# Windowed attention with sink keys, then routed experts: scores and V products in four 64x64 tiles over the halves of keys that each half of queries sees

## The chip, the cores and the metric

One core of a Trainium2 chip runs the whole program. The time is that of the device for one execution, in microseconds; the kernel before has 536.01 us as the median of 3 runs. In the profile PE is TensorE's matrix product, PEld its weight loads, DVE is VectorE, ACT is ScalarE, POOL is GpSimd and SP is SyncE, which issues most DMAs.

## What is computed

There are 4 batches, 8 heads, 768 positions and 64 elements in a head. A query sees the first 4 keys (the sinks) and the 128 keys up to itself. The attention's output is regrouped to 3072 tokens of 512 elements, and each token goes through the one expert of 8 that its largest gate logit names.

```python
scores = scale * np.matmul(q, k.transpose(0, 1, 3, 2))
is_sink = pos[None, :] < int(n_sink)
rel = pos[:, None] - pos[None, :]
in_window = (rel >= 0) & (rel < int(window))
scores = np.where(is_sink | in_window, scores, -1000000000.0)
...
out = np.matmul(a, v)                  # a: softmax of the scores
...
logits = x @ w_gate
e_idx = np.argmax(logits, axis=1)
...
h = np.maximum(x[mask] @ w1[e], 0.0)
out[mask] = gate_w[mask, None] * eom[mask, e, None] * (h @ w2[e])
```

## The kernel before

Two heads of a batch make a pair (index `a` in the code); there are 16 pairs, and `pair(p)` records one. Its 128 partitions hold head 0 in the lower half and head 1 in the upper. The 768 positions are six tiles of 128 queries.

For each tile `t`, `score(t)` (line 1227) has TensorE compute the scores of 128 queries against 260 key columns: 128 of the tile before, 4 sinks, 128 of its own tile. Tile 0 needs 132 columns. Each head is one matmul in a 64-row tile of the array, all 128 queries wide, plain fp32 (which the engine runs as two instructions). `fold` on VectorE (lines 1234 to 1239) puts the scores of the tile before into the places of the own tile's future keys and takes the row maximum; `exps` on ScalarE (line 1243) takes the exponentials, 132 columns a head. `trans(j)` transposes two tiles of them on TensorE (line 1267), ScalarE copies them out of PSUM (line 1270) into `f`, and GpSimd splits them by two selects into `f` (keys of the own tile) and `g` (keys of the tile before).

`av(kt)` (line 1318) is the V product of one tile of keys: its `f` part goes to the queries of tile `kt`, its `g` part to those of tile `kt + 1`, with all 128 keys as rows and a 64-column tile of the array for each head. The outputs of query tiles 0 to 3 lie in the PSUM bank `oA`, those of 4 and 5 in `oB`. The sinks go a way of their own: GpSimd packs their exponentials (line 1287), TensorE transposes them (1293), ScalarE rounds them to the fast fp32 form (1302) and VectorE takes what rounding left (1296); three DMAs put high, high and low parts on 24 rows of `psk` (1306), which `av_sink` (1330) multiplies by a likewise split copy of the sink values, `vst` (1199, 1200, once a batch). ScalarE then copies `oA` and `oB` to `ot` (1334, 1335); the gate product (1340) writes into the rest of `oB` and is copied to `lgT` (1344); `ot` is transposed back and divided by the row sums (1380, 1383).

After each batch VectorE routes its tokens. Four early expert slots take full slots of the batches that are done, the first in plain fp32 (line 1057), the others with weights split in high and low parts (1076, 1114). Thirteen more follow when all batches are routed. Weights come in chunks of 512 KB.

No loop runs on the chip in this part: a planner (`Plan.order`) decides the order of every engine's instructions before. Each step has an engine, a guessed length, its dependences and a due number, which is the pair's base plus the table `AT`, or the entry of the table `PIN` for that step alone. On each engine the step that can start first goes, and among those near it the one with the smallest due number. `SWITCH` is the planner's guess for TensorE's change of tile shape, `SOFT` how far a plain expert step may be put off. What the planner puts out is fixed; on the chip each engine goes through its own list and waits on semaphores. The score buffers are two (`s0`, `s1`), so the scores of tile `t + 2` wait for the exponentials of tile `t`.

Of the kernel before, what the change touches and what calls it, by code (L numbers as in the profile page):

```python
# [8 lines left out]
F32 = mybir.dt.float32  # L9
# [41 lines left out]
SOFT = 11611  # L51
# [5 lines left out]
    "load": -121675, "v": -30283, "vs": 194803, "sinkv": -43076, "scale0": 12478, "scale1": -125988, "scale2": 94931,  # L57
    "s0": 3034, "s1": 8110, "s2": 8849, "s3": 12417, "s4": 3772, "s5": 8559, "fold": -17871, "exp": 28702,
    "tr0": 32076, "tr1": 44886, "tr2": 55920, "trc": 52551, "mask": 31852, "pack": -44418, "guard": -99464,
# [72 lines left out]
}  # L132


# [1526 lines left out]
```

## Time and profile before

| what | value |
|---|---|
| median of 3 runs | 536.01 us (535.85 to 536.72) |
| profiled execution | 534.44 us, its span 532.6 us |
| TensorE granted clock, mean | 0.990 |
| busy: PE, PEld, DVE, ACT, POOL | 500.5, 389.9, 346.3, 283.0, 196.6 us |
| moved | 113.01 MB, mean 212 GB/s |

A record of the profile lasts from an instruction's start until its result has landed, so a matmul's record holds the drain of the array, and records of one block lie over each other. Attention lasts until about 200 us: the last score matmul starts at 185.1 us. A timeline row merges neighbouring records of one line (x4 is four of them); one plain fp32 matmul makes two records. A row's bracket says how long the engine was idle before it and what ended that.

### The profile page before, as it was taken

What the parts mean: (1) busy time and instruction counts of PE and PEld (TensorE: products, weight loads), DVE (VectorE), ACT (ScalarE), POOL (GpSimd) and SP (SyncE); (2) the same over time, 40 slices, a digit from 0 to 9 for tenths busy, and PEclk for the clock granted to TensorE, in tenths of its full rate; (3) what the DMA queues carried; (4) which work ended last, traced back from release to release, by engine and by line L of the source; (5) the groups of instructions that cost most, each with busy time, mean ns of one, the idle gap of its engine ahead of it and who ended that gap; (6) DMA issues with size and microseconds to landing.
All of it is one profiled execution on the core that took longest, in us unless ns stands there. A gap on an engine that the chain in (4) does not pass through costs nothing.

```text
span 532.6 us, 10377 instructions
## 1 busy us (share of the span) xinstructions
PE 500.5 (94%) x3501; PEld 389.9 (73%) x3501; DVE 346.3 (65%) x800; ACT 283.0 (53%) x741; POOL 196.6 (37%) x298
## 2 busy tenths in 40 slices
PE   8799999998899989997999899999998999999992
PEld 3556676666566766687898898979886986988861
DVE  6567788788876495979999752163546578274530
ACT  4477777676756544763545432261626567365420
POOL 8675867767683253024053203040205012001101
PEclk9899999999999999999999899999999999999998
DMA  8454456536991219594385834865499979984860
GB/s 268 113 166 149 157 161 185 159 109 226 387 333 49 61 46 298 186 313 176 120 303 187 286 113 153 311 238 179 156 352 343 293 271 293 380 279 147 287 231 21
DMA packets 62687, 113.01 MB, mean 212 GB/s; under 512 B 8188, under 2 KB 28928, under 8 KB 62626
## 3 DMA queue, kind: packets, MB, share of 16 engines
q1 hardware_dynamic: 58162, 98.13, 54.5%
q0 software_dynamic: 4464, 14.14, 7.7%
q8 instruction: 30, 0.49, 0.4%
q14 instruction: 31, 0.25, 0.1%
HBM read 98.48 MB, written 13.44 MB: 210 GB/s over the span
## 4 chain that ended last, share of the span: by engine, by line
PE 43%; issue 25%; DVE 10%; DMA 8%; POOL 6%; ACT 4%; SPq 1%; POOLq 0%; another core or an unknown queue 0%; ACTq 0%; DVEq 0%
PE s L1076 13%; PE oA L1114 7%; PE oB L1114 5%; PE s L1227 5%; DMA q<-in_qT_dram 3%; PE oA L1318 3%; PE tp L1267 2%; ACT e L1243 2%; POOL out_dram L970 2%; DMA v<-in_vx_dram 2%; DMA raw<-in_w_dram 2%; PE s L1057 2%; POOL xg L892 2%; PE tp L1380 1%; DMA xg<-xd,idx_e 1%
## 5 line engine op out<-in xcount | busy, mean ns | idle before, releaser
L1243 ACT ACTIVATE e<-s,nmx 128x132 f32<-128x132 f32 x192 | 69.7, 371 | 37.8 <-DVE nmx L1239 28.4
L970 POOL DMA_INDIRECT out_dram<-y,idx x20 | 20.9, 1043 | 137.1 <-ACT y L967 133.7
L1227 PE MATMUL s<-k,q 64*128 64x260 f32 (+1 forms) x384 | 65.4, 412 | 4.9 <-ACT e L1243 4.4
L988 ACT ACTIVATE hh<-s 128x512 fp32r<-128x512 f32 (+1 forms) x36 | 23.2, 644 | 74.8 <-PE s L1076 65.8
L991 DVE SCALAR_TENSOR_TENSOR hl<-s,hh 128x512 fp32r<-128x512 f32 (+1 forms) x36 | 26.9, 747 | 50.7 <-ACT hh L988 50.7
L892 POOL DMA_INDIRECT xg<-xd,idx x21 | 27.5, 1309 | 85.0 <-PE tp L952 45.3
L1227 PEld LDWEIGHTS s<-k,q 64*128 64x128 f32 x384 | 33.4, 189 | 22.5 <-ACT e L1243 15.0
L1236 DVE COPY_PREDICATED s<-maskf,s 128x256 f32<-128x256 int32 x80 | 33.8, 423 | 17.9 <-PE s L1227 13.0
L1239 DVE TENSOR_REDUCE nmx<-s 128x2 f32<-128x264 f32 x96 | 41.5, 432 | 3.3
L1208 POOL TENSOR_SCALAR q<-q 128x256 f32<-128x256 f32 x45 | 38.0, 861 | 7.7 <-DMA q<-in_qT_dram 2.7
L383 POOL TENSOR_SCALAR_AFFINE_SELECT g<-f 128x512 f32<-128x512 f32 (+1 forms) x48 | 26.9, 560 | 33.1 <-ACT f L1270 33.0
L1243 ACT ACTIVATION_READ_ACCUMULATOR e<-s,nmx 128x1 f32 x192 | 38.8, 202 | 0.0
L1270 ACT COPY f<-tp 128x512 f32<-128x512 f32 x48 | 28.0, 588 | 11.0 <-PE tp L1267 10.9
L1267 PE MATMUL tp<-ident,e 128*128 128x128 f32 x192 | 30.1, 284 | 0.9 <-DVE x L1383 0.7
L1318 PE MATMUL oA<-f,v 128*64 128x128 f32 x256 | 26.8, 288 | 2.7 <-DMA v<-in_vx_dram 2.7
L383 POOL TENSOR_SCALAR_AFFINE_SELECT f<-f 128x512 f32<-128x512 f32 (+1 forms) x48 | 27.7, 576 | 3.3
L1267 PEld LDWEIGHTS tp<-ident,e 128*128 128x128 f32 x192 | 21.5, 143 | 9.5 <-issue 2.7
L1318 PEld LDWEIGHTS oA<-f,v 128*64 128x64 f32 x256 | 14.5, 137 | 11.9 <-issue 8.3
L967 ACT ACTIVATE y<-oA,sc 128x512 f32<-128x512 f32 (+1 forms) x18 | 11.7, 650 | 20.3 <-PE oA L1114 14.8
L970 POOL DMA_INDIRECT out_dram<-y,idx_e x8 | 9.9, 1242 | 32.1 <-ACT y L967 30.5
L1318 PE MATMUL oA<-g,v 128*64 128x128 f32 x192 | 18.9, 276 | 0.0
L931 DVE TENSOR_TENSOR wa1l<-raw,wa1h 128x1024 fp32r<-128x1024 f32 x11 | 13.4, 1223 | 7.5 <-ACT wa1h L927 7.4
(550 smaller groups left out, 1530.9 us busy)
## 6 DMA issues: line engine op xcount, KB each, us to landing
raw<-in_w_dram SPq DMA_DIRECT2D x96, 512.0 KB
v<-in_vx_dram SPq DMA_DIRECT2D x8, 768.0 KB
xd<-x SPq DMA_DIRECT2D x16, 384.0 KB
k<-in_kx_dram SPq DMA_DIRECT2D x15, 396.0 KB
q<-in_qT_dram SPq DMA_DIRECT2D x15, 384.0 KB
wa0h<-in_w_dram SPq DMA_DIRECT2D x3, 512.0 KB
wa0l<-in_w_dram SPq DMA_DIRECT2D x3, 512.0 KB
wa3h<-in_w_dram SPq DMA_DIRECT2D x3, 512.0 KB
```

Source lines behind the costliest of these rows:

```text
L383: nc.gpsimd.affine_select(out=ap, in_=ap if src is None else src, pattern=pattern, compare_op=op, fill=fill, base=base, channel_multiplier=cm)
L892: nc.gpsimd.indirect_dma_start(out=p.get(key), out_offset=None, in_=xd[0:n + 1, :], in_offset=bass.IndirectOffsetOnAxis(ap=ids(), axis=0))
L970: nc.gpsimd.indirect_dma_start(out=where, out_offset=bass.IndirectOffsetOnAxis(ap=ids(), axis=0), in_=p.get(yk)[:, 0:m], in_offset=None, b ...
L1076: nc.tensor.matmul(out=p.get(ps)[:, j, 0:cols], lhsT=a, rhs=p.get(x)[:, d, 0:cols], start=d == 0 and i == 0, stop=d == ND - 1 and i == 2)
L1114: nc.tensor.matmul(out=p.get(ys[s]), lhsT=h[a][:, s * P:(s + 1) * P], rhs=w[b_], start=f == 0 and i == 0, stop=f == NF - 1 and i == len(th ...
L1208: (nc.gpsimd if p else nc.vector).tensor_scalar(out=c, in0=c, scalar1=SCALE, scalar2=None, op0=ALU.mult)
L1227: nc.tensor.matmul(out=get(s)[:, a, o0:P + CW], lhsT=get(q)[r, t * P:(t + 1) * P], rhs=get(k)[r, k0:k0 + P + CW - o0], start=True, stop=True)
L1236: nc.vector.copy_predicated(out=both[:, :, 4:CW], mask=bc(maski[:, 1, 4:CW], 1, 2), data=z[:, :, 0:P])
L1239: nc.vector.tensor_reduce(out=get(nmx)[:, t, :], in_=both, axis=AX.X, op=ALU.max, negate=True)
L1243: nc.scalar.activation(out=get(e)[:, t, a, :], in_=get(s)[:, a, P:P + CW], func=AF.Exp, bias=get(nmx)[:, t, a:a + 1], scale=1.0, accum_out ...
L1267: nc.tensor.transpose(out=get(tp)[:, i, :], in_=get(e)[:, 2 * j + i // 2, i % 2, 4:CW], identity=ident)
L1318: nc.tensor.matmul(out=o, lhsT=v_[:, kt, p % 2 * P + a * D:p % 2 * P + (a + 1) * D], rhs=src[:, kt, a, :], start=t == kt == 0 or t == kt + ...
```

## The change

`score` computes each tile with t > 0 in four 64x64 tiles of the array, two heads by two halves of 64 queries, and over 196 columns each: the lower half of queries leaves out the upper 64 keys of its own tile, and the upper half the lower 64 of the tile before. The score buffers become two lasting PSUM tiles, written once at the start.

The V product has rows of 64 keys. Each tile of keys gives `f` and `g` products for each half of keys; two of these four cover all 128 queries and two only the 64 that see the half. A query tile with an even number now lies in `oA`, one with an odd number in `oB`, three of each. The products go in six parts: three "even" ones, in which the lower half of rows writes `oA` and the upper `oB`, then three "odd" ones the other way round. Between them ScalarE copies one column of `oB` to `tick`, after the even parts; the odd parts wait for it.

The sinks stay plain fp32: two packings, two transpositions, one copy of 256 columns, two DMAs, and four products of 384 columns in 64x64 tiles. The low part and its VectorE steps go, and the sink values are loaded straight into `vst`. The gate product writes both banks, three matmuls of 128 columns in each. All of `AT` and `PIN` are new, and `SWITCH` and `SOFT` with them.

```diff
-SOFT = 11611
+SOFT = 12779
...
-    "load": -121675, "v": -30283, "vs": 194803, "sinkv": -43076, "scale0": 12478, "scale1": -125988, "scale2": 94931,
+    "load": -118603, "v": -35855, "vs": 192361, "scale0": 15699, "scale1": -134944, "scale2": 109581, "s0": 1473,
...
-    SWITCH = {"row": 200}
+    SWITCH = {"four": 170}
...
+        class Held:
+            def __init__(self):
+                self.tiles = {}
+            def tile(self, shape, dt, name):
+                if name not in self.tiles:
+                    self.tiles[name] = ps.tile([P, 2, 512], F32, name=name)
+                t = self.tiles[name]
+                return t if len(shape) == 3 else t[:, 0, :]
...
-                nc.vector.tensor_copy(out=vst[0:24], in_=get(vsr))
-                tt(out=vst[0:8], in0=get(vsr)[0:8], in1=vst[0:8].bitcast(F32), op=ALU.subtract)
+                    def sink_values(r=slice(i * D, i * D + 2 * SINK)):
+                        nc.sync.dma_start(out=vsts[b % 2][r], in_=vs[b, 0:2 * SINK])
...
-                    for a in range(2):
-                        r = slice(a * D, (a + 1) * D)
-                        nc.tensor.matmul(out=get(s)[:, a, o0:P + CW], lhsT=get(q)[r, t * P:(t + 1) * P],
-                                         rhs=get(k)[r, k0:k0 + P + CW - o0], start=True, stop=True)
+                    for h in range(2):
+                        c0, c1 = (o0, P + CW) if t == 0 else (0, P + CW - D) if h == 0 else (D, P + CW)
+                        for a in range(2):
+                            r = slice(a * D, (a + 1) * D)
+                            nc.tensor.matmul(out=get(s)[h * D:(h + 1) * D, a, c0:c1], lhsT=get(q)[r, t * P + h * D:t * P + (h + 1) * D],
+                                             rhs=get(k)[r, k0 + c0 - o0:k0 + c1 - o0], start=True, stop=True)
...
-            pl.op("DVE", fn=sink_lo, r=[st_, (hl, 0)], w=[(hl, 1)], at=(at, "lo"), **dve(128))
-            for j, w in enumerate((0, 0, 1)):
+            for j in range(2):
...
+            parts = [("even", 0, 1), ("even", 2, 3), ("even", 4, 5), ("odd", 4, 5), ("odd", 0, 1), ("odd", 2, 3)]
+            def av(i):
+                side, *kts = parts[i]
+                todo, ks = [], set()
+                for kt in kts:
+                    whole = (kt % 2 == 0) == (side == "even")
+                    for h, src, t in ((0, "f", kt), (1, "g", kt + 1)) if whole else ((0, "g", kt + 1), (1, "f", kt)):
+                        if t < T:
+                            todo.append((h, src, kt, t, (0, P) if whole else ((0, D), (D, P))[h]))
...
+                    for h, src, kt, t, (c0, c1) in todo:
+                        rows_ = slice(h * D, (h + 1) * D)
+                        for a in range(2):
+                            o = get((oA, oB)[t % 2])[a * D:(a + 1) * D, t // 2, c0:c1]
...
+                    pl.op("ACT", fn=lambda: nc.scalar.copy(out=get(tick), in_=get(oB)[:, 2, 0:1]), r=[oA, oB, ("av", p, 1), ("av", p, 2)],
+                          w=[tick], at=(at, "tick"), **act(1))
...
-                for o, t0, t1 in ((get(oA)[:, 1:4, :], 0, 3), (get(oB)[:, 0:2, :], 3, 5)):
-                    nc.tensor.matmul(out=o, lhsT=vsts[b % 2][:, hp, :], rhs=psks[p % 2][:, t0:t1, :],
+                for r, o in ((slice(0, D), oB), (slice(D, P), oA)):
+                    for a in range(2):
+                        c = slice(a * D, (a + 1) * D)
+                        nc.tensor.matmul(out=get(o)[c, 0:3, :], lhsT=vsts[b % 2][r, hp, c], rhs=psks[p % 2][r],
```

The order, too, is another. TensorE's list of the kernel before, from the last two of the nine groups of one pair's V product (1318) and its sinks (1330) on; line 1227 is the scores, 1293 the sinks' transposition, 1380 that of `ot`, 1340 the gate product:

```order
L1318 MATMUL oB<-g_587,v_238 64x128 x2
L1318 MATMUL oB<-f_582,v_238 64x128 x2
L1330 MATMUL oA<-psk_189,vst_190 128x384
L1330 MATMUL oB<-psk_189,vst_190 128x256
L1227 MATMUL s_768<-k_490,q_481 128x132 x2
L1227 MATMUL s_774<-k_490,q_481 128x260 x2
L1293 MATMUL tp_783<-ident,pk_772 40x128
L1380 MATMUL tp_785<-ident,ot_777 128x128 x4
L1318 MATMUL oA<-f_726,v_238 64x128 x2
```

The same list of the kernel after, around the step from even to odd parts of one pair; its line 1335 is the V product, 1232 the scores, 1272 the transposition of exponentials:

```order
L1335 MATMUL oA<-f_450,v_240 64x128 x2
L1335 MATMUL oB<-g_468,v_240 64x128 x2
L1335 MATMUL oB<-f_450,v_240 64x64 x2
L1232 MATMUL s_212<-k_234,q_229 64x196 x4
L1272 MATMUL tp_655<-ident,e_530 128x128 x4
L1232 MATMUL s_209<-k_345,q_342 64x132 x4
L1335 MATMUL oB<-g_468,v_240 64x64 x2
L1335 MATMUL oA<-f_450,v_240 64x64 x2
L1335 MATMUL oB<-f_450,v_240 64x128 x2
```

The V product that ran through without a break is cut in two, and two score blocks and a transposition stand in the cut.

ScalarE's list of the kernel after at the same place; line 1248 is the exponentials, 1275 the copy of transposed ones, 1348 the tick:

```order
L1248 ACTIVATE e_530,rs_531<-s_209,nmx_512 128x132 x2
L1348 COPY tick_664<-oB 128x1
L1275 COPY f_636<-tp_655 128x512
L1248 ACTIVATE e_530,rs_531<-s_212,nmx_512 128x132 x2
L1248 ACTIVATE e_708,rs_709<-s_209,nmx_682 128x132 x2
```

The tick, which the list before does not have, stands behind one pair of exponentials and ahead of the copy and the exponentials that answer to the work in the cut.

SyncE's list of the kernel before, up to the first weight load of the first early slot; `q`, `k`, `v` are queries, keys and values, line 1306 sends the packed sinks, `order_i` names the expert:

```order
L1185 DMA q_1824<-in_qT_dram 128x768
L1185 DMA k_1831<-in_kx_dram 128x792
L1306 DMA psk_189<-hlk_1887 8x5x128 x3
L1190 DMA v_1932<-in_vx_dram 128x6x256
L897 TENSOR_LOAD order_i
L897 ISA x2
L915 ISA
L915 DMA wa0h<-in_w_dram 128x1024
```

And of the kernel after, up to the same load; line 1313 sends the packed sinks, 1421 stores an output:

```order
L1313 DMA psk_189<-hlk_2284 8x3x128 x2
L895 TENSOR_LOAD order_i
L895 ISA x2
L1421 DMA xd<-x_2320 128x6x128
L1191 DMA q_2377<-in_qT_dram 128x768
L1191 DMA k_2379<-in_kx_dram 128x792
L913 ISA
L913 DMA wa0h<-in_w_dram 128x1024
```

The loads of one more pair's queries and keys now stand ahead of those weights. Before, the loads of two pairs stood behind all eight of them, now those of one.

## Rows read from the trace of the kernel before

**Rows 1.** Windows, whole core: length, PE, PEld, DVE, ACT, POOL busy, clock, DMA.

```profile
20.00:120.00 100.00, 95.87 (x925) 64.43 (x924) 77.32 (x221) 72.20 (x301) 68.35 (x121) 1.00 0.47 146
120.00:160.00 40.00, 35.81 (x348) 24.47 (x349) 32.27 (x97) 26.09 (x110) 30.46 (x50) 1.00 0.91 315
...
300.00:500.00 200.00, 198.42 (x1151) 170.71 (x1149) 105.70 (x128) 96.52 (x138) 32.06 (x27) 1.00 0.72 254
```

**Rows 2.** Timeline (start, length, engine): TensorE around one V product.

```profile
107.12 0.66 PE L1267 MATMUL tp<-ident,e 128*128 128x128 f32 x4
...
107.70 0.71 PE L1227 MATMUL s<-k,q 64*128 64x260 f32 x4
...
108.34 0.20 PEld L1318 LDWEIGHTS oA<-f,v 128*64 128x64 f32 x4 [0.34 <-issue]
108.34 0.44 PE L1318 MATMUL oA<-f,v 128*64 128x128 f32 x4
...
108.61 0.39 PE L1318 MATMUL oA<-g,v 128*64 128x128 f32 x4
108.72 0.25 PEld L1318 LDWEIGHTS oA<-f,v 128*64 128x64 f32 x4
...
108.83 0.39 PE L1318 MATMUL oA<-f,v 128*64 128x128 f32 x4
...
109.05 0.39 PE L1318 MATMUL oA<-g,v 128*64 128x128 f32 x4
...
109.38 0.30 PEld L1227 LDWEIGHTS s<-k,q 64*128 64x128 f32 x4 [0.18 <-ACT e L1243]
```

**Rows 3.** Waits of weight loads, 20 to 200: total, times, longest.

```profile
PEld s L1227 <- ACT e L1243: 13.6, 35, 1.2
...
PEld tp L1293 <- POOL pk L1287: 3.4, 6, 1.1
```

**Rows 4.** Timeline: the two sink products of one pair.

```profile
101.01 0.44 PE L1330 MATMUL oA<-psk,vst 64*128 64x384 f32 x1
...
101.29 0.28 PE L1330 MATMUL oB<-psk,vst 64*128 64x256 f32 x1
```

**Rows 5.** Timeline, 101 to 105: the steps that change on other engines.

```profile
101.27 0.24 POOL L1287 COPY pk<-e 128x40 f32<-128x40 f32 x1
...
101.61 0.41 DVE L1199 CAST vst<-vsr 24x512 fp32r<-24x512 f32 x1
...
102.05 0.68 DVE L1200 TENSOR_TENSOR vst<-vsr,vst 8x512 fp32r<-8x512 f32 x1
...
102.49 0.26 ACT L1302 CAST hlk<-tp 40x128 fp32r<-40x128 f32 x1
...
102.77 2.33 SPq L1306 DMA_DIRECT2D psk<-hlk  x3
...
103.50 0.37 ACT L1344 COPY lgT<-oB 96x256 f32<-96x256 f32 x1 [0.76 <-PE oB L1340]
...
104.12 0.27 DVE L1296 TENSOR_TENSOR hlk<-tp,hlk 40x128 fp32r<-40x128 f32 x1
```

**Rows 6.** Timeline: one pair of exponentials on ScalarE.

```profile
108.48 0.40 ACT L1243 ACTIVATE e<-s,nmx 128x132 f32<-128x132 f32 x1
...
108.83 0.40 ACT L1243 ACTIVATE e<-s,nmx 128x132 f32<-128x132 f32 x1
...
109.09 0.24 ACT L1243 ACTIVATION_READ_ACCUMULATOR e<-s,nmx 128x1 f32 x1
```

**Rows 7.** Windows of line 1227 alone: length, PE busy (records), PEld.

```profile
20.00:120.00 100.00, 39.89 (x236) 20.26 (x236) 1.00 0.47 146
```

**Rows 8.** Chain of waits, 126 to 160: start, length; then TensorE's timeline before 18.

```profile
134.14 9.93 DMA q<-in_qT_dram
...
16.67 0.69 PE L1318 MATMUL oA<-f,v 128*64 128x128 f32 x4 [2.71 <-DMA v<-in_vx_dram]
```

More of the change, by code (lines that the diff above doesn't have):

```diff
@@ L1172, in idle, with begin @@
                 nc.tensor.matmul(out=pl.get(spare), lhsT=ones, rhs=bc(ones, 1, 4), start=True, stop=True)
-        pl.op("PE", 2400, lambda: idle(7), w=[spare], at=-1000000, mode="full", busy=2400)
+        whole = [new(pl, "s", [P, 2, 512], key=("warm", i)) for i in range(2)]
+        def begin():
+            for t in whole:
+                for i in range(2):
+                    nc.tensor.matmul(out=pl.get(t)[:, i, :], lhsT=ones, rhs=bc(ones, 1, 4), start=True, stop=True)
+            idle(3)
+        pl.op("PE", 2400, begin, w=[spare, *whole], at=-1000000, mode="full", busy=2400)
         def pair(p):
@@ L1282, in pair, with pack, fn @@
                 trans(j)
-            pk, hl = new(pl, "pk", [P, 2, SINK, T - 1], key=("pk", p)), new(pl, "hlk", [8 * (T - 1), 2, P], F32R, key=("hlk", p))
-            st_, n = new(pl, "tp", [P, P], key=("sk", p)), 8 * (T - 1)
-            def pack():
-                nc.gpsimd.tensor_copy(out=get(pk), in_=get(e)[:, 1:T, :, 0:4].rearrange("p t a s -> p a s t"))
+            n = SINK * T
+            pk = new(pl, "pk", [P, 2, n], key=("pk", p))
+            hl, st_ = new(pl, "hlk", [n, 2, P], key=("hlk", p)), new(pl, "tp", [P, 2, P], key=("sk", p))
+            def pack(j):
+                def fn():
+                    nc.gpsimd.tensor_copy(out=get(pk)[:, j, :].rearrange("p (a s t) -> p a s t", a=2, s=SINK),
+                                          in_=get(e)[:, 1 - j:T:2, :, 0:SINK].rearrange("p t a s -> p a s t"))
+                pl.op("POOL", fn=fn, r=[(e, t) for t in every], w=[(pk, j)], at=(at, "pack"), took=250, busy=420)
             def guard():
@@ L1292, in turn_sink @@
             def turn_sink():
-                nc.tensor.transpose(out=get(st_)[0:n, :], in_=get(pk).rearrange("p a s t -> p (a s t)"), identity=ident)
-            def sink_lo():
-                tt(out=get(hl)[:, 1, :], in0=get(st_)[0:n, :], in1=get(hl)[:, 0, :].bitcast(F32), op=ALU.subtract)
+                for j in range(2):
+                    nc.tensor.transpose(out=get(st_)[0:n, j, :], in_=get(pk)[:, j, :], identity=ident)
             every = range(T)
-            pl.op("POOL", fn=pack, r=[(e, t) for t in every], w=[pk], at=(at, "pack"), took=250, busy=420)
+            for j in range(2):
+                pack(j)
@@ L1308, in pair, with send @@
+            pl.op("ACT", fn=lambda: nc.scalar.copy(out=get(hl), in_=get(st_)[0:n]), r=[st_], w=[hl], at=(at, "hl"), **act(256))
+            for j in range(2):
+                def send(j=j):
+                    nc.sync.dma_start(out=psks[p % 2][j * D:j * D + 2 * SINK], in_=get(hl)[:, j, :])
+                pl.op("SP", 2000, send, r=[hl], w=[(("psk", p % 2), j)], at=(at, "send"), size=20000, busy=790)
             pl.op("DVE", fn=lambda: nc.vector.reciprocal(out=get(rs), in_=get(rs)), r=[(rs, "g")], w=[(rs, "r")], at=(at, "recip"), **dve(12))
@@ L1324, in pair @@
-            for kt in range(T):
-                av(kt)
+            parts = [("even", 0, 1), ("even", 2, 3), ("even", 4, 5), ("odd", 4, 5), ("odd", 0, 1), ("odd", 2, 3)]
[7 more added lines that the diff above has]
+                            todo.append((h, src, kt, t, (0, P) if whole else ((0, D), (D, P))[h]))
+                            ks.add(((f, g)[src == "g"], t // 2))
+                def fn():
+                    for h, src, kt, t, (c0, c1) in todo:
+                        rows_ = slice(h * D, (h + 1) * D)
+                        for a in range(2):
+                            o = get((oA, oB)[t % 2])[a * D:(a + 1) * D, t // 2, c0:c1]
+                            nc.tensor.matmul(out=o, lhsT=get(v)[rows_, kt, p % 2 * P + a * D:p % 2 * P + (a + 1) * D],
+                                             rhs=get((f, g)[src == "g"])[rows_, kt, a, c0:c1], start=i == 0 and kt == 0,
+                                             stop=False, skip_group_check=True)
+                ks = sorted(ks, key=str)
+                cost = pe(325, "four")
+                if i == 0:
+                    return pl.op("PE", fn=fn, r=ks + [v], w=[oA, oB], at=(at, "av0"), **cost)
+                return pl.op("PE", fn=fn, r=ks + [v] + [("tick", p)] * (i > 2), w=[("av", p, i)], hold=[oA, oB], behind=begun, at=(at, "av%d" % i), **cost)
@@ L1326, in pair @@
+            begun = [av(0)]
+            for i in range(1, 6):
+                if i == 3:
+                    tick = new(pl, "tick", [P, 1], key=("tick", p))
+                    pl.op("ACT", fn=lambda: nc.scalar.copy(out=get(tick), in_=get(oB)[:, 2, 0:1]), r=[oA, oB, ("av", p, 1), ("av", p, 2)],
+                          w=[tick], at=(at, "tick"), **act(1))
+                begun[1:] = [av(i)]
             ot = new(pl, "ot", [P, T, P], key=("ot", p))
             def av_sink():
-                for o, t0, t1 in ((get(oA)[:, 1:4, :], 0, 3), (get(oB)[:, 0:2, :], 3, 5)):
-                    nc.tensor.matmul(out=o, lhsT=vsts[b % 2][:, hp, :], rhs=psks[p % 2][:, t0:t1, :],
-                                     start=False, stop=True, skip_group_check=True)
@@ L1333, in pair @@
[L1333 to L1335 removed]
+                for r, o in ((slice(0, D), oB), (slice(D, P), oA)):
+                    for a in range(2):
+                        c = slice(a * D, (a + 1) * D)
+                        nc.tensor.matmul(out=get(o)[c, 0:3, :], lhsT=vsts[b % 2][r, hp, c], rhs=psks[p % 2][r],
+                                         start=False, stop=True, skip_group_check=True)
@@ L1336, in pair @@
+            pl.op("PE", fn=av_sink, r=[(("vst", b % 2), i) for i in range(2)] + [(("psk", p % 2), j) for j in range(2)] + [("av", p, i) for i in range(1, 6)],
+                  w=[oA, oB], at=(at, "avs"), **pe(650, "four"))
+            for j, o in enumerate((oA, oB)):
+                pl.op("ACT", fn=lambda j=j, o=o: nc.scalar.copy(out=get(ot)[:, j:T:2, :], in_=get(o)[:, 0:3, :]), r=[o], w=[(ot, j)], at=(at + 10 * j, "ot"),
+                      **act(384))
             lgT = new(pl, "lgT", [96, 2, P], key=("lgT", p))
@@ L1338, in gate1 @@
             def gate1():
-                for j in range(3):
-                    nc.tensor.matmul(out=get(oB)[32 * j:32 * j + 32, 2:4, :], lhsT=wgt[:, hp, :], rhs=get(ot)[:, j:j + 4:3, :],
-                                     start=True, stop=True, skip_group_check=True)
-            pl.op("PE", fn=gate1, r=["wgt", (ot, 0), (ot, 1)], w=[oB], at=(at, "g1"), **pe(450, "quad"))
-            pl.op("ACT", fn=lambda: nc.scalar.copy(out=get(lgT), in_=get(oB)[0:96, 2:4, :]), r=[oB], w=[lgT], at=(at, "lgT"), **act(256))
+                for i, o in enumerate((oA, oB)):
+                    for j in range(3):
+                        nc.tensor.matmul(out=get(o)[32 * j:32 * j + 32, 3, :], lhsT=wgt[:, hp, :], rhs=get(ot)[:, 3 * i + j, :],
+                                         start=True, stop=True, skip_group_check=True)
@@ L1345, in pair @@
+            pl.op("PE", fn=gate1, r=["wgt", (ot, 0), (ot, 1)], w=[oA, oB], at=(at, "g1"), **pe(450, "quad"))
+            for i, o in enumerate((oA, oB)):
+                pl.op("ACT", fn=lambda i=i, o=o: nc.scalar.copy(out=get(lgT)[:, i, :], in_=get(o)[0:96, 3, :]), r=[o], w=[(lgT, i)], at=(at, "lgT"), **act(128))
             gt, lw = new(pl, "tp", [P, 4, P]), new(pl, "lw", [P, T, 2, 2 * E])
```

52 lines of the change are left out of this document (18 added, 34 removed), and 122 rows, old and new, of tables (AT, PIN).

## The prediction

> **What bounds the kernel now.** I read the table by stretches first [rows 1]. Attention over 16 pairs of heads fills the first 200 us, the expert layer the rest. From 20 to 120 us TensorE is busy 95.87 of 100 us; VectorE has 77.32, ScalarE 72.20, GpSimd 68.35. After 300 us it is busy 198.42 of 200 us. So TensorE is the first suspect everywhere, but a busy matmul row is not a streaming one, so I read a stretch of its timeline next [rows 2]. In a V product four records (two column tiles, each matmul two instructions) start 0.22 us after the four before them (108.61, 108.83, 109.05), and a record of 128 columns lasts 0.39. Streaming is thus 0.217 us for 128 columns of plain fp32, or 1.70 ns a column, with the tiles running side by side; the other 0.17 us of a record is the drain, hidden until the block ends.
>
> It is not hidden where the tile shape changes. A score block starts at 107.70 and the V product's first weights at 108.34: 0.64 us, of which 260 x 1.70 ns = 0.44 stream, so 0.20 us go to weights at its head and the drain at its end. The V block from 108.34 to 109.38 has four groups, 0.87 us, and 0.17 left. Four transpositions of 0.109 take 107.12 to 107.70: 0.44 and 0.14. These visits are the second term of the sum. Waits for others are the third: the longest kind that names an engine's work, score weights waiting for ScalarE's exponentials, is 13.6 us in 180, and the next 3.4 [rows 3].
>
> **The change part by part.** All times are against the profiled execution (span 532.6, own time 534.4 us); the median of the runs is 536.0, so I add 1.6 at the end.
>
> *Scores.* Of 96 blocks the 80 with t > 0 go from 260 to 196 columns per tile: 64 x 1.70 ns = 0.109 us less, 8.7 us in all. The 16 blocks of t = 0 keep 132 columns. This needs all four 64x64 tiles to stream at once. The trace shows two row tiles at once (four score records in 0.71 us, drain included) and two column tiles at once, never both; I take full overlap because each of the two runs at 1.70 ns a column alone.
>
> *V products.* Before, 11 groups a pair: 2.39 us. After, six parts with at most 192 columns on a tile: 6 x 0.326 = 1.96 us if each part waits for its longer tile, 1088 columns or 1.85 us if the last two run into each other. Gain 0.43 to 0.54 a pair, 6.9 to 8.6 in all; I take 7.5.
>
> *Sinks.* Before, 384 and 256 columns of one instruction each: the second starts 0.28 us after the first and the pair is about 0.28 us of array [rows 4]. After, 384 columns at 1.70 ns: 0.65. That is 0.37 a pair, 6.0 us added. A second transposition of packed sinks adds 0.109 a pair, 1.7 us. The gate product keeps its columns. Streaming together: -8.7 - 7.5 + 6.0 + 1.7 = **-8.5 us**.
>
> *Changes of tile shape.* Scores, V products and sinks now share one shape, so going from one to another needs no drain. Counted along TensorE's order between the first and the last attention row, there were 185 changes: 71 into the row shape, 33 into the column shape, 65 into the full array, 16 into the gate's shape. Now there are 152: 65 into the four-tile shape, 71 full, 16 gate. Priced by the visits above: 71 x 0.20 + 33 x 0.17 + 65 x 0.14 = 28.9 us before. A four-tile visit isn't in the trace; it loads 64 columns of weights like the V block, so I take 0.16: 65 x 0.16 + 71 x 0.14 = 20.3. With 0.20 it would be 22.9, with 0.14, 19.0. Gain **-8.6 us**, bounds 6.0 to 9.9.
>
> *The new wait.* The odd parts of V now wait for a one-column copy ("tick") on ScalarE that itself waits for the even parts. Its price: drain 0.17 [rows 2], the copy at most the 0.26 of a 128-column copy [rows 5], and 0.05 back to TensorE (ScalarE's accumulator read ends at 109.33, the score weights start at 109.38) [rows 2, 6]: 0.48 us. If an exponential pair stands ahead on ScalarE, its 0.85 us (108.48 to 109.33) come on top [rows 6]: 1.33. Against that, TensorE's order has work between the parts: in 3 of 16 pairs one block (0.33 us for a score), in 13 two or more, mostly a score and four transpositions, about 1.0 us. So from 0 to 1.0 us a pair; most pairs are near the covered end, and I take 0.2: **+3.2 us**. What is queued behind a late tick: the exponentials of the next scores, and behind those, with two score buffers, the scores.
>
> *Other engines.* VectorE loses the low-half subtraction (0.27 a pair) and the two sink-value instructions (0.41 + 0.68 a batch) [rows 5]. ScalarE gains: sink copy 128 to 256 columns (about 0.26 to 0.37), gate copy split (two of 0.26 for one of 0.37), tick (0.26): 0.52 a pair. GpSimd packs twice: +0.24. SyncE sends two DMAs for three (2.33 us for three), so 0.78 less. Are they covered? 236 score records in 100 us are 9.8 pairs [rows 7], 10.2 us a pair; the forecast takes 0.87 off, 9.3. ScalarE then holds 7.4 + 0.5 = 7.9 us (85%), VectorE 7.9 - 0.5 = 7.4 (79%), GpSimd 7.0 + 0.2 = 7.2 (77%). All fit, none by much; if the cover goes, the price is a rival below.
>
> *Order of loads.* The chain of waits passes through a query load of 9.93 us that stood behind 4 MB of expert weights [rows 8]; two pairs' loads stood behind them, now one does. In 120 to 160 us TensorE is idle 4.19 us in 40, where the rate of 20 to 120 gives 1.65 [rows 1], so 0 to 2.5 us may come back. The first V load, for which TensorE waited 2.71 us [rows 8], is issued earlier: 0 to 2.7. I count nothing for either, as another load may be the late one, and keep both for the low end.
>
> *The expert layer.* It keeps its instructions. Its weight buffers open when attention's pools close, and the last routing follows the last pair, so both move with the end of attention. Four early expert slots cover the routing as before. I count nothing.
>
> Sum: -8.5 - 8.6 + 3.2 = -13.9; 534.4 - 13.9 + 1.6 = **522.1 us**.
>
> **A rule that speaks against it.** The V rows load four sets of weights over all 128 rows in each 0.22 us, and the 0.22 is the columns alone: weights for a later matmul load beside the running one, on the same rows [rows 2]. Exposed weights would cost 0.05, the excess of a block's first group (0.44) over a later one (0.39). The Trainium skill (TensorE: Matmul & The Clock Gate, Part 3: Packing small matmuls) says that a weight load overlaps a running matmul only where its row group differs. This trace disagrees for column tiles; of four tiles no run here shows it. If weights were exposed there, some 24 V groups and 6 second score halves a pair would pay 0.05 each, 1.5 us a pair, 24 us: 546.
>
> **The rivals.** *The other engines take over.* With ScalarE at 85% and every queue in order, half the gain goes into longer waits: about 529. For it: the share of each engine rises to some 80%. Against: VectorE gets relief and named waits are small now. *The tick decides.* If it comes behind an exponential pair each time (1.0 us a pair) and its late release delays the next exponentials as well, the wait counts twice: 32 us against the 17.1 of the other terms, 551, slower than before. It turns slower where the whole wait passes 1.07 us a pair. Against: the work placed between the parts. *Four tiles don't overlap* and run two by two: scores 80 x 0.33 + 16 x 0.22, V 16 x 1.96, sinks 16 x 0.65 more, 72 us: 594. Against: both kinds of overlap are there singly. *The loads help too:* tick hidden, 2.5 and 2.7 us back: 514, and 516 with most of it.
>
> **How the numbers follow.** Forecast 0.62 (522.1, within 518 to 527), loads help 0.11, other engines 0.15, tick 0.07, exposed weights 0.03, no overlap 0.02. This case's measurement can tell about 0.2%, 1.1 us, from no change. Faster is the first three less the far end of the third: 0.85; same 0.03; slower 0.12. Range: down to 513, where streaming and shapes are at their best (-9.6 and -9.9) and part of the loads' 5.2 us comes back, up to 533, where a tick of 0.9 us a pair leaves 2.7 us of gain. That leaves out the slower cases and a little at either end.
>
> **What would show it.** Score blocks of eight records at two times 0.16 us with starts a few ns apart; V parts 0.33 us apart without a drain towards a score; TensorE waits on the tick's line under 5 us in all; attention's last sink product some 13 us earlier and the first expert slots moved by the same. I am wrong if records of the four tiles start one after another, if waits for the exponentials grow past 20 us, or if attention ends early and the gap before the late experts widens.

## The result, and the profile after

The kernel after takes **513.89 us** (median of four runs, 512.22 to 516.02), the kernel before 535.93 beside it: a ratio of 0.960, with a 95% interval of 0.955 to 0.965. The forecast was 522.1 with a range of 513 to 533, so the time lies in the range, close to its low end; 22.0 us were gained where 13.9 were forecast. The profiled execution of after took 513.68 us, with a span of 511.9.

Windows of after, the stretches of [rows 1] (columns as there):

```profile
20.00:120.00 100.00, 95.72 (x1930) 69.66 (x1924) 81.42 (x234) 79.21 (x348) 76.31 (x146) 1.00 0.54 169
120.00:160.00 40.00, 37.70 (x684) 25.41 (x678) 30.54 (x91) 31.15 (x136) 31.02 (x55) 1.00 0.75 268
...
300.00:500.00 200.00, 198.43 (x1163) 164.34 (x1162) 101.43 (x112) 96.65 (x140) 34.15 (x31) 1.00 0.75 258
```

From 20 to 120 us TensorE's busy share is what it was (95.9 to 95.7), and from 120 to 160 it rose by 1.9 us. The three other engines hold 4 to 8 us more of each 100 than before, since the same work of theirs stands in less time. Where the pairs end is read from the sink products, one per pair. Here are the groups of that tile, of before and then of after: duration in ns (least, median, most), first and last start in us.

```profile
L1330 PE MATMUL oB<-psk,vst x16: 271/276/284, 26.0 to 199.4; 64*128 64x256 f32 x16
```

```profile
L1357 PE MATMUL oB<-psk,vst x64: 482/482/533, 24.6 to 182.1; 64*64 64x384 f32 x64
```

Attention's last sink product starts 17.3 us sooner (199.4 to 182.1). What is left of the span behind it goes from 333.2 to 329.8 us: 3.4 us more come from the expert layer.

Next the timeline of TensorE in after, with a score block between transpositions and around one score block and one V product, for comparison with [rows 2]:

```profile
15.27 0.56 PE L1232 MATMUL s<-k,q 64*64 64x196 f32 x8
15.76 0.54 PE L1303 MATMUL tp<-ident,pk 128*24 128x128 f32 x2
...
67.92 0.56 PE L1232 MATMUL s<-k,q 64*64 64x196 f32 x8
...
68.30 0.27 PE L1335 MATMUL oA<-f,v 64*64 64x128 f32 x1
68.30 0.13 PEld L1335 LDWEIGHTS oA<-f,v 64*64 64x64 f32 x1
...
68.31 0.27 PE L1335 MATMUL oB<-g,v 64*64 64x128 f32 x1
...
68.63 0.27 PE L1335 MATMUL oA<-f,v 64*64 64x128 f32 x1
...
80.62 0.54 PE L1357 MATMUL oB<-psk,vst 64*64 64x384 f32 x2
...
81.32 0.94 PE L1232 MATMUL s<-k,q 64*64 64x196 f32 x16
```

The score block's eight records end 0.56 us after its start, where four records of 260 columns took 0.71. It and the V product behind it have one shape, and the V product starts 0.38 us after the block did: 0.33 of columns and no drain between them. A block that stands between transpositions takes 0.49 us up to the next of them (15.27, 15.76): 0.16 more than its columns. One V part to the next is 0.33 us (68.30, 68.63), and tiles of different rows and columns start 5 to 10 ns apart. So four tiles stream at once at 1.70 ns a column. The sink product takes 0.70 us up to the next score (80.62 to 81.32), 0.65 of it columns.

Waits of TensorE's weight loads in after, 20 to 200 us (total, times, longest), for [rows 3]:

```profile
PEld s L1232 <- ACT e L1248: 11.0, 30, 1.2
...
PEld oA L1370 <- ACT ot L1363: 2.9, 11, 0.5
```

And the tick, the copy that the odd V parts wait for, by its tile:

```profile
L1348 ACT COPY tick<-oB x16: 156/159/180, 22.5 to 180.5; 128x1 f32<-128x1 f32 x16
...
  PEld oB L1335: 0.9, 3
  PEld s L1232: 0.7, 4
  PE oB L1335: 0.2, 1
```

It takes 0.16 us, and TensorE waits 1.8 us for it in all, over the 16 pairs (the last three lines are who waited for it).

### The profile page after: what moved, and what is told of

It reads as the page before. It is cut to its first block, busy times and chain, and to the rows that moved or that the text cites. A ratio compares the mean times of both kernels' runs of the same rounds, so it can differ in the third digit from the quotient of the medians.

```text
span 511.9 us, 12956 instructions
## 1 busy us (share of the span) xinstructions
PE 486.7 (95%) x4797; PEld 384.0 (75%) x4797; DVE 335.1 (65%) x776; ACT 285.0 (56%) x773; POOL 196.1 (38%) x314
## 4 chain that ended last, share of the span: by engine, by line
PE 56%; issue 16%; DVE 12%; DMA 7%; ACT 5%; POOL 2%; another core or an unknown queue 0%; POOLq 0%; ACTq 0%; DVEq 0%
PE s L1074 14%; PE oA L1112 9%; PE oB L1112 7%; DMA raw<-in_w_dram 7%; PE s L1232 6%; PE tp L1272 3%; PE s L1055 3%; PE oA L1335 3%; PE oB L1335 2%; ACT e L1248 2%; PE tp L1411 2%; PE s L1087 2%; DVE nmx L1244 2%; DVE s L1241 1%; POOL out_dram L968 1%
## 5 line engine op out<-in xcount | busy, mean ns | idle before, releaser
L890 POOL DMA_INDIRECT xg<-xd,idx x21 | 24.5, 1168 | 93.3 <-PE tp L950 77.9
L1232 PE MATMUL s<-k,q 64*64 64x196 f32 (+1 forms) x768 | 51.8, 341 | 6.6 <-ACT e L1248 6.1
L1232 PEld LDWEIGHTS s<-k,q 64*64 64x64 f32 x768 | 23.3, 133 | 26.0 <-ACT e L1248 15.7
L1335 PE MATMUL oB<-g,v 64*64 64x128 f32 (+1 forms) x384 | 32.0, 248 | 0.2 <-ACT tick L1348 0.2
L1335 PE MATMUL oB<-f,v 64*64 64x64 f32 (+1 forms) x384 | 31.0, 244 | 0.0
L1335 PE MATMUL oA<-f,v 64*64 64x128 f32 (+1 forms) x384 | 30.6, 251 | 0.3 <-POOL f L367 0.3
L1272 PEld LDWEIGHTS tp<-ident,e 128*128 128x128 f32 x192 | 20.8, 141 | 9.3 <-issue 2.4
L965 ACT ACTIVATE y<-oA,sc 128x512 f32<-128x512 f32 (+1 forms) x18 | 11.7, 651 | 23.6 <-PE oA L1112 18.0
L1335 PEld LDWEIGHTS oB<-g,v 64*64 64x64 f32 x384 | 23.0, 133 | 2.1 <-issue 1.0
```

The source lines that it names most:

```text
L1232: nc.tensor.matmul(out=get(s)[h * D:(h + 1) * D, a, c0:c1], lhsT=get(q)[r, t * P + h * D:t * P + (h + 1) * D], rhs=get(k)[r, k0 + c0 - o0: ...
L1272: nc.tensor.transpose(out=get(tp)[:, i, :], in_=get(e)[:, 2 * j + i // 2, i % 2, 4:CW], identity=ident)
L1335: nc.tensor.matmul(out=o, lhsT=get(v)[rows_, kt, p % 2 * P + a * D:p % 2 * P + (a + 1) * D], rhs=get((f, g)[src == "g"])[rows_, kt, a, c0: ...
```

## The experiments

My first theory was that of the sum: in attention TensorE's own time sets the pace, so each term comes through nearly one for one. The rivals were that part of it is taken up by waits, and that the order made anew, or the place of the loads in it, carries part of the gain. In the first two experiments the order of every engine is that of the kernel they start from.

**Scores alone in the kernel before** (its order and all else kept; the score buffers are held, so that columns that no tile writes have been written once):

```diff
-                    for a in range(2):
-                        r = slice(a * D, (a + 1) * D)
-                        nc.tensor.matmul(out=get(s)[:, a, o0:P + CW], lhsT=get(q)[r, t * P:(t + 1) * P],
-                                         rhs=get(k)[r, k0:k0 + P + CW - o0], start=True, stop=True)
+                    for h in range(2):
+                        c0, c1 = (o0, P + CW) if t == 0 else (0, P + CW - D) if h == 0 else (D, P + CW)
+                        for a in range(2):
...
```

> The kernel before with only its scores in four 64x64 tiles, in the order of before. First theory (TensorE's array time is on the path nearly one for one): 80 blocks lose 0.109 us of streaming, 8.7 us; shape changes stay about equal (70 at 0.16 and 16 at 0.20 us for 71 at 0.20), so about 527 us. Rival (the old order hands the gain to the waits for ScalarE's exponentials, and only the new order turns it into time): less than 4 us, 532 to 536.

Measured 532.52 us (ratio 0.9931, 0.9893 to 0.9970): 3.7 us gained, with 1.6 to 5.7 as the interval, of the 8.7 that the columns are worth. The first theory is out, and the rival's "less than 4" fits. Its waits, 20 to 200 us:

```profile
PEld s L1251 <- ACT e L1267: 15.2, 37, 1.0
...
PEld tp L1317 <- POOL pk L1311: 4.7, 5, 1.8
```

Both are longer than in [rows 3]. In an order made for slower scores, part of what TensorE saves is waited for again.

**Scores back in two tiles in the kernel after**, the reverse edit, with after's order:

> The kernel after with its scores back in two 64x128 tiles over 260 columns, in the order of after. First theory: 8.7 us of streaming come back, and scores and V products no longer share a shape: 218 changes in place of 152 (84 to the row shape at 0.20 and 47 to the four-tile shape at 0.16 for 65 at 0.16), 13.9 us; together 22.6, about 536 us. Rival (the new order carries the gain, TensorE has slack): plus 5 to 12 us, 519 to 526.

Measured 528.42 us (0.9834, 0.9786 to 0.9882), 12.6 us above after by the two ratios. That is more than the 8.7 of the columns, just above the rival's 5 to 12, and less than the 22.6 of the full theory. In the profiled execution attention's last sink product starts 16.8 us later than in after (198.9 for 182.1); TensorE's columns and the gaps of up to 0.22 us at its shape changes take some 17 us more up to there, and its longer waits hardly change. So what is added to TensorE does come through in attention, and some 3 us of it are won back behind. Together the two runs say that the scores in four tiles matter, and that what they give depends on the order around them.

**A wider tick** (384 columns in place of one):

```diff
-                    tick = new(pl, "tick", [P, 1], key=("tick", p))
+                    tick = new(pl, "tick", [P, 3, P], key=("tick", p))
...
-                    pl.op("ACT", fn=lambda: nc.scalar.copy(out=get(tick), in_=get(oB)[:, 2, 0:1]), ...
+                    pl.op("ACT", fn=lambda: nc.scalar.copy(out=get(tick), in_=get(oB)[:, 0:3, :]), ...
```

> The kernel after with a longer tick: ScalarE copies all 384 columns of oB, about 0.49 us for 0.16, in the same order. If the tick is covered by the work between the parts: 0 to 2 us more, 514 to 516. If the wait for it is on the path: 0.33 us in each of 16 pairs, 5.3 us, about 519 us.

Measured 515.57 us (0.9574, 0.9531 to 0.9618), which can't be told from after. The tick's tile in this kernel:

```profile
L1348 ACT COPY tick<-oB x16: 473/479/499, 25.1 to 186.6; 128x384 f32<-128x384 f32 x16
...
  PEld oB L1335: 2.7, 7
  PE oB L1335: 1.0, 3
```

The copy grew by 0.32 us, 5.1 us over the pairs, and TensorE's waits for it by 1.9. The tick is covered, and so is most of a further 5 us of ScalarE's time.

**A third of the sinks' columns:**

```diff
-                        nc.tensor.matmul(out=get(o)[c, 0:3, :], lhsT=vsts[b % 2][r, hp, c], rhs=psks[p % 2][r],
+                        nc.tensor.matmul(out=get(o)[c, 0, :], lhsT=vsts[b % 2][r, hp, c], rhs=psks[p % 2][r, 0, :],
```

> The kernel after with each sink product over 128 columns in place of 384, so two thirds of the sinks' part are left out; same order. First theory: 0.65 us becomes 0.22 in 16 pairs, 6.9 us less, about 507 us. Rival (the sink products stand where TensorE waits anyway): 0 to 2 us less, 512 to 514.

Measured 513.79 us (0.9547, 0.9504 to 0.9591): between nothing (by the medians) and 2.8 us (by the ratios) of the 6.9 us that left the array. Its waits, 20 to 200 us:

```profile
PE s L1232 <- ACT e L1248: 5.0, 15, 1.0
```

In after the same line is 2.8 us, 8 times, and the one of the weight loads grew from 11.0 to 12.6. More of the score blocks stand there waiting for a buffer that the exponentials still read. It is so behind the first 30 us too (12.1 for 9.8, and 4.6 for 2.8), so a lower clock around 20 us, on which more at the end, doesn't make it. Here the theory of one for one fell: in this order array time taken off one product gives little.

**No mask in the folds.** If the array isn't the limit, the loop of score, fold, exponentials through two score buffers could be:

```diff
-                    else:
+                    elif t == 1:
                         nc.vector.copy_predicated(out=both[:, :, 4:CW], mask=bc(maski[:, 1, 4:CW], 1, 2), data=z[:, :, 0:P])
```

> The kernel after, with the copy under the mask left out of the folds of blocks 2 to 5 of each pair (64 VectorE instructions of 0.44 us between a score block and its maximum; the scores of the two windows are not merged there, so the outputs are not attention's). Same order on the other engines. It asks what bounds the new kernel in the attention part, after a third of the sinks' array time off gave nothing. Theory A: the loop score, fold, exponentials through the two score buffers ends last: TensorE's waits for a score buffer (11 to 14 us before 200 us) shrink by a third or more, and the time falls by 4 to 10 us: 504 to 510. Theory B: ScalarE's queue with its order is the limit, so a shorter fold is waited for behind other work of ScalarE: the time falls by 0 to 2 us: 512 to 514. Theory C: TensorE's own time is the limit after all: no change, waits as before, 513 to 515.

Measured 512.32 us (0.9587, 0.9547 to 0.9626): 0.6 to 1.6 us less. Windows and waits (20 to 200) of this kernel:

```profile
20.00:120.00 100.00, 97.06 (x1923) 71.27 (x1922) 64.23 (x192) 79.46 (x347) 76.60 (x147) 0.97 0.53 167
```

```profile
PEld s L1232 <- ACT e L1249: 6.0, 16, 0.8
```

VectorE lost 17 of 81 us in this stretch and the waits for the exponentials nearly halved (11.0 to 6.0), and still the time moved little: part of theory A (the waits), the result nearer to B. The granted clock accounts for some of it: 0.97 here against 1.00, most of it in 20 to 27 us, where the windows give 0.51. Between runs of about one mean clock the gain is 2 to 4 us: 513.89 at 0.979 beside after's 516.02 at 0.980, 509.79 at 0.987 beside 514.10 at 0.985. Neither 7 us taken off the array, 5 us put on ScalarE nor 27 us taken off VectorE (64 x 0.42) is worth more than some 4 us. In this order, relieving one engine alone gives little, while work added to TensorE lengthened attention by about as much as was added (the scores in two tiles).

**No numbers of their own for single steps.** What is the fitted order worth? `PIN` gives single steps a due number (536 before, 405 after), beside the numbers of `AT` for a class of steps. In these two it is empty, and `AT` is each kernel's own:

```diff
-PIN = {
...
-}
+PIN = {}
```

> The kernel before without the table PIN, so its order comes from the table AT alone. To be read against the next run: if the tiles make the gain, before and after without their pins differ by as much as with them, 20 us or more; if the pinned order makes about half of it, by 8 to 14 us. Its own time: 540 to 560 us, as the pins hold single steps where waits were.

> The kernel after without the table PIN. Theory of the tiles: 20 us or more under the kernel before without its pins. Theory of the order (half of the gain is the due numbers of single steps): 8 to 14 us under it.

Before went to 559.59 us (1.0431, 1.0378 to 1.0485), after to 553.83 (1.0325, 1.0261 to 1.0389). So the gain shrinks from 22 us to 5.8, less than either theory had. The spans and the sinks of the two, before first:

```profile
core 0 of [0], span 560.4 us
...
L1330 PE MATMUL oB<-psk,vst x16: 271/276/284, 27.5 to 210.6; 64*128 64x256 f32 x16
```

```profile
core 0 of [0], span 551.7 us
...
L1357 PE MATMUL oB<-psk,vst x64: 482/482/533, 28.5 to 198.0; 64*64 64x384 f32 x64
```

In attention the change still gives 12.6 us (210.6 to 198.0), and some 11 of them are TensorE's columns and its gaps of up to 0.22 us. Behind it after is 3.9 us *longer* (349.8 to 353.7), where with `PIN` it is 3.4 shorter. TensorE's granted clock is the same in both (0.96 from 20 to 198 us, 0.98 from 210 to 530). Most of attention's gain is thus there without numbers for single steps; the expert part's, and some 5 us of attention's, are not.

**The expert steps' due numbers exchanged**, after with before's, and before with after's (attention's steps keep their own; the index moves by the 16 ticks):

```diff
-PIN = {i: own}
+PIN = {i: own for attention's steps, other[i - 16] for the expert steps}
```

> The kernel after, but the expert steps have the due numbers that the kernel before pins for the same steps; attention's steps keep theirs. If the experts' new order gives the 3 to 4 us by which the time behind attention's last sink product shrank (333.4 to 330.2 us of span): 517 to 520 us. If that came with attention's earlier end: 513 to 515 us.

> The kernel before, but the expert steps have the due numbers that the kernel after pins for the same steps. If the experts' new order is worth 3 to 4 us by itself: 532 to 534 us. If it fits only the new attention: 536 us or more, since weights and early slots then come at other times than the old attention leaves room for.

After with the old ones: 539.75 us (1.003, 0.9988 to 1.0072). Its runs spread from 533 to 541 us; the best of them is still 19 us above after, so nearly all of the gain is lost, far outside both theories. Before with the new ones: 537.38 (1.0027, 0.9999 to 1.0055), nothing won, as the second theory said. Its sinks and its span:

```profile
core 0 of [0], span 535.4 us
...
L1330 PE MATMUL oB<-psk,vst x16: 271/276/278, 26.5 to 204.7; 64*128 64x256 f32 x16
```

Its attention ends 5.3 us later than before's own (199.4) and the rest of the span is 2.5 us shorter: 2.5 us more of expert columns lie among the pairs, and about that is given back behind. So the experts' new due numbers are worth nothing by themselves, and the new attention little where the experts' don't fit it. One can't be priced without the other.

**The loads.** The forecast had put two loads at 0 and kept 5.2 us for them at the low end; the time came out where they would have brought it. Three kernels move loads in SyncE's queue and nothing else. The core of the edit, here for the first of them:

```diff
-        for _, i in self.order():
-            self.ops[i]["fn"]()
+        out = [i for _, i in self.order()]
...
+        for moved, to, off in ((loads(14), weights[7], 1),):
+            for i in moved:
+                out.remove(i)
+            n = out.index(to) + off
+            out[n:n] = moved
+        for i in out:
+            self.ops[i]["fn"]()
```

After, with the last pair but one's query and key loads late:

> The kernel after, with one change in SyncE's queue alone: the query and key loads of the last pair but one (0.8 MB) stand behind seven of the eight weight loads (3.5 MB) of the first early expert slot, near to where the kernel before has them. All other instructions stand in the same order. This asks what the new place of these loads is worth. Theory of the prediction's sum (loads count nothing): 513 to 515 us, as another wait takes the place. Theory that the loads give what they cost the kernel before (up to 2.5 us there): 515.5 to 517. Theory of the fitted order: in the trace of after GpSimd scales that pair's first queries at 122.2 us, 4 us after their load was issued, and its queue is in order; 3.5 MB at the 0.4 MB a us of that stretch put the load some 9 us later, so GpSimd and the score behind it wait up to 8 us there: 518 to 522.

Measured 525.61 us (0.9818, 0.9790 to 0.9847), 11.7 above after, more than any theory had. The chain of waits, GpSimd's timeline, TensorE's, and the windows:

```profile
125.44 10.32 DMA q<-in_qT_dram
...
135.91 0.85 POOL q L1224
136.76 0.60 POOL g L380
```

```profile
135.91 0.85 POOL L1224 TENSOR_SCALAR q<-q 128x256 f32<-128x256 f32 x1 [11.06 <-DMA q<-in_qT_dram]
...
137.41 0.37 PE L1348 MATMUL oA<-g,v 64*64 64x64 f32 x2 [10.03 <-POOL g L380]
```

```profile
120.00:160.00 40.00, 28.48 (x460) 18.63 (x462) 23.92 (x69) 22.93 (x103) 22.93 (x41) 0.83 0.74 254
```

The late queries hold GpSimd for 11.06 us, the masks of *another* pair stand behind them in its queue, and TensorE waits 10.03 us for a mask. Then it runs at the lower clock level up to 143.1 us. This is the third theory at a higher price.

Before, with the first V load and that pair's loads early:

> The kernel before, with both loads that the prediction's low end named moved to the front in SyncE's queue alone: the first V load ahead of the second pair's keys and the third pair's loads (it is the tenth load of the start otherwise, and TensorE waits 2.71 us for it), and the query and key loads of the last pair but one ahead of the eight weight loads of the first early slot (4 MB; the chain of waits passes through 9.93 us of this query load). Everything else stands as before. The forecast counted 0 for both, as another load or wait may be the late one: 535 to 537 us. If both ends of the price are real, 2.7 + 2.5 us come back: 530.5 to 532, and the same 5 us would explain the waits that the kernel after lost beyond the sum. If the gain is 1 to 3 us only, 533 to 535, the loads explain part.

Measured 543.31 us (1.0161, 1.0134 to 1.0188): not 5 us less but 8.6 more, outside all three, and its last sink product starts 8.6 us later (208.0). At the start the V load's wait is gone (the first V product at 14.09 us in place of 16.67), and others are there, listed for 0 to 30 us:

```profile
PE tp L1306 <- POOL pk L1300: 1.8, 1, 1.8
...
PE s L1240 <- POOL q L1221: 0.9, 1, 0.9
PE s L1240 <- DMA k<-in_kx_dram: 0.8, 1, 0.8
```

They add up to 3.5 us, where 2.7 were saved. Later, SyncE's timeline, and one wait of TensorE (100 to 210 us):

```profile
127.76 0.40 SPq L1203 DMA_DIRECT2D v<-in_vx_dram  x1
134.66 0.34 SPq L1198 DMA_DIRECT2D q<-in_qT_dram  x1
...
135.68 0.35 SPq L928 DMA_DIRECT2D wa0h<-in_w_dram  x1
...
146.29 3.36 SPq L1319 DMA_DIRECT2D psk<-hlk  x3
```

```profile
PE oA L1343 <- DMA psk<-hlk: 4.8, 1, 4.8
```

In before's own order the weights are issued from 128.93 us. Here they stand behind the query load, which isn't issued until 134.66 (SyncE waits 4.5 us for scores that still read its buffer), so the sinks' sends move behind a later burst of weights (146.29; 141.87 in before), and TensorE waits 4.8 us for one. A load that is moved to the front takes its own wait with it.

After, with the third pair's V load behind the first pair's:

> The kernel after, with one load moved: the V load of the third pair (768 KB), which stands third in SyncE's queue at the start, goes behind the V load of the first pair, the tenth. Nothing else moves. In the trace of after the chain of waits at the start passes through the third pair's query load, landed at 18.43 us, GpSimd's scaling of it, then the mask that the first V product waits for (0.31 us) and the score waits before it (1.68 and 0.57 us of TensorE). 768 KB at 0.4 MB a us is 1.9 us, so these queries land about 1.9 us sooner. Theory that the start is on the path: 1 to 2 us less, 512 to 513, beside 513.9. Theory that a wait further on takes it up, as with the loads counted at nothing: 513.5 to 514.5. Slower than 515 only if the first pair's V, now sooner, or the third pair's V, now later, is needed before it lands.

Measured 517.99 us (0.9671, 0.9641 to 0.9700), 4 us slower than after, outside both theories. The queries did land sooner (GpSimd scales the first at 7.56 us, 9.42 in after). Then, in the chain of waits, and TensorE's timeline:

```profile
9.56 6.22 DMA nsw_i<-in_window_dram
15.88 0.18 DVE nswf L447
```

```profile
15.25 0.56 PE L1245 MATMUL s<-k,q 64*64 64x196 f32 x8
18.94 0.93 PE L1245 MATMUL s<-k,q 64*64 64x196 f32 x8 [3.12 <-ACT e L1261]
```

VectorE's queue holds a conversion of a small load (nsw_i) ahead of the folds. It now ends last, 0.5 us later than in after, and the next score waits. The idle stretch is one of 3.12 us in place of 1.68, and from 18.6 to 25.4 us the granted clock is 0.50. Getting there sooner only made the wait longer. Part of the 4 us goes with the clock: all six runs have a mean of 0.979 to 0.985, and after's own run at 0.980 took 516.02 us.

## Why the prediction was right, and where not

**Streaming (forecast -8.5): right in parts, too good in sum.** I added up TensorE's records of attention up to the last sink product in both traces, each with its columns at their rate. Scores gave -8.5 (forecast -8.7), the V products -6.8 (-7.5; the low bound was 6.9), the second sink transposition +1.7 as forecast, the sinks +7.5 (+6.0). The step that failed for the sinks is the price of before's pair: I took the 0.28 us between two starts [rows 4] as array time. After's pair is 0.65 as forecast, so +7.5 leaves 0.18 for before's. In the 0.28 the second product's weights are loaded (101.12 to 101.31), and a score streams beside the sinks on the other rows:

```profile
101.03 0.49 PE L1227 MATMUL s<-k,q 64*128 64x132 f32 x2
```

All of attention's columns together: -5.7.

**Shape changes (forecast -8.6, bounds 6.0 to 9.9): right, at the low bound.** The gaps of up to 0.22 us between these streams went from 30.2 to 24.1 us: -6.2. So a visit of four tiles costs about as much as any other (0.16 us at 15.27, as I had taken), and the gain is that there are fewer.

**The two together** are -11.9 where 17.1 were forecast. The pair of kernels without `PIN`, with 12.6 us in attention, agrees.

**The tick (+3.2): too dear.** 1.8 us of waits, and tripling the copy's time changed nothing that can be told: 0. The mechanism was right (work placed between the parts covers it), only most pairs are at the covered end altogether.

**Waits of others and loads (0): too careful, and for a wrong reason.** Gaps over 0.22 us in attention shrank from 23.0 to 18.6, and gaps at the expert steps among the pairs by 2.8. The 2.71 us for the first V load [rows 8] are gone. But my reason for that was wrong: what after issues earlier is the third pair's V load, and the first pair's stands tenth of the loads (eleventh before, with that of the sink values). The wait is gone because four more score blocks stand ahead of the first V product, which starts at 20.69 us. The rival "the loads help too" gave 514 and the time is 513.9, yet it is not what happened: the two loads that I had named, moved by themselves, made before 8.6 us slower. Taking the early place of the last pair but one away cost after 11.7 us, since in its order the mask of another pair stands behind that pair's queries.

**Other engines (half the gain lost): no.** The shares came out at 79, 81 and 76% (forecast 85, 79 and 77), and waits for exponentials fell from 13.6 to 11.0 us.

**The expert layer (0): wrong by 3.4 us.** I had held that it moves as a block with attention's end. It doesn't: without `PIN` its part grows by 3.9, with it it shrinks by 3.4. Most of the 3.4 are waits: behind the last sink product TensorE is busy 317.0 us in before and 316.3 in after, and idle 16.2 and 13.6.

**The rule against it.** The Trainium skill (TensorE: Matmul & The Clock Gate, Part 3: Packing small matmuls) says that a weight load overlaps running matmuls only where its row group differs, so by it weights would be exposed where tiles share rows. In after the four weight loads of the second V group lie beside the first group's matmuls (68.30 to 68.32), and the next group starts 0.11 us after it, which is its columns' time. This trace disagrees for four tiles too. The same section's span of a pack is one matmul's duration and about 4 ns for each further tile; the starts here, 5 to 10 ns apart, are near it.

In balance, profiled execution against profiled execution (534.4 to 513.7, -20.8): -5.7 and -6.2 for columns and shapes, -4.4 for the longer waits with the tick's among them, and -4.3 for the expert steps (+1.9 of their work and -2.8 of their gaps among the pairs, -3.4 behind) make -20.6. The forecast had -8.5, -8.6, +3.2 and 0. It was 5.2 too hopeful on the tiles and some 12 too careful on everything else. The likeliest case's own range of 518 to 527 missed the time, the wider range held it by 0.9 us. That is luck in part: its low end stood on streaming and shapes at their best, 19.5 us, and they gave 11.9; the error on the tiles and the larger one the other way partly cancel. What stays open is how the 4.4 us of waits and the 4.3 us of the expert steps divide among single steps of the order: taking one load's place back (11.7 us) or the experts' due numbers (over 19) cost more than these 8.7, so they can't be added up. Open, too, is what a newly fitted order would bring the old tiles: no run gives before's attention one.

## What to carry to other kernels

Price a shape change by what streams and by how many visits are left, and both are read from one stretch of a timeline. In a kernel whose order is fitted to its durations, don't price a moved load or a shorter step alone: half of a saving can be waited for again in the old order, work taken off one engine can count for little where work added counts in full, and a piece of a new order in an old kernel can cost more than it was to bring. When an in-order queue gets an instruction earlier, ask what *it* waits for and what then stands behind it, as in the queues of SyncE, GpSimd and VectorE here.

## What the runs showed of the hardware

Four 64x64 tiles of plain fp32 stream at once at the rate of one (1.70 ns a column), with starts 5 to 10 ns apart and their weights loaded beside. And an idle stretch of TensorE could have a second price: after 10.03 us of waiting in one kernel and 3.12 us in another the granted clock was 0.50, the 1.2 GHz level, for the work that followed, and a score block took 0.93 us there in place of 0.56. The length of the wait doesn't decide it alone. In the profiled execution of after, 1.68 us of waiting at the same place were followed by a granted clock of 1.00; with the wide tick the same 1.68 us were followed by 0.50 from 20 to 27 us, and with a third of the sinks' columns by 0.50 from 20 to 22 us. The block behind the wait in that last kernel:

```profile
18.36 0.93 PE L1232 MATMUL s<-k,q 64*64 64x196 f32 x8 [1.68 <-ACT e L1248]
```

With the scores alone, 2.43 us of waiting before 15.87 were followed by 1.00. The four runs of after differ in the same way: with mean clocks of 0.992, 0.991, 0.985 and 0.980 they took 512.22, 513.68, 514.10 and 516.02 us. What decides between the two levels at that place stays open.
